# Three of the seven loads of the first double chunk issued from ScalarE's DMA queue

## The chip, the cores and the metric

The kernel runs on one core of a Trainium2 chip. The core has a matrix engine (TensorE, PE in the profile, with PEld for its weight loads), a vector engine (VectorE, DVE), an activation engine (ScalarE, ACT), a general engine (GpSimd, POOL) and a queue engine without arithmetic (SyncE, SP). Each takes its own instructions in program order and waits for the others on semaphores. Transfers between device memory and on-chip memory are issued by an engine's sequencer (SPq, ACTq, POOLq in the profile) and carried out by 16 DMA engines, which the core's queues share. The metric is device microseconds of one execution; lower is better.

## The reference

Two layers follow each other: a gated linear attention, and a feed-forward layer with a squared ReLU.

```python
batch, n_heads, seq, head_dim = (4, 8, 768, 48)     # q, k, v, alpha
n_tokens, d_model, d_ff = (3072, 384, 2048)
for t in range(S):
    state = alpha[:, :, t, :, None] * state + np.einsum('bhd,bhe->bhde', k[:, :, t], v[:, :, t])
    y[:, :, t] = np.einsum('bhd,bhde->bhe', q[:, :, t], state)
...
x = y.transpose(0, 2, 1, 3).reshape(B * S, H * D)
h = x @ w_in
r = np.maximum(h, 0.0)
return (r * r) @ w_out
```

All inputs and the output are float32.

## The kernel before

The 3072 tokens are 24 chunks of 128, six to a batch. For a chunk the attention is written with matrix products: the logarithm of alpha is summed along the chunk by a product with a triangular matrix, its exponentials A and 1/A (tiles `A` and `Ainv`) scale q and k, the scaled q and k are transposed, their product is masked and multiplied by v, and a running state (`st`, its copy `sb`) carries what earlier chunks left. The result `xn` is transposed into `xT_big`, from which the feed-forward layer reads: a first product (`w_in_b`), ReLU on ScalarE (`r`), square on VectorE (`gT`), a second product (`w_out_b`), copy and store.

The first four chunks are done as two double chunks (function `add_super`, u = 0 and 1), since they have nothing to hide behind. A double chunk reads `at` (alpha), `qt` and `kt` as two halves each, of four heads (`ld_at0`, `ld_at1` and so on, v = 0 and 1), and `vt` whole: seven loads, six of 192 KB and one of 384 KB. Function `add_load2` makes them. The first half of the heads goes through: logarithm (line 646, ScalarE), cumulative product p0 (PE), `A` and `Ainv` (line 682, ScalarE), the two scalings into `qk_s` (line 698, VectorE: q, then k), transposes p1 (line 276, PE), copy to `qkT` (line 396, VectorE), the masked scores `sm` (line 761, VectorE); the second half follows in the same way, and `vb` is the cast of `vt` (line 654, GpSimd). The state is advanced by the product `st` (PE) and its scaling at line 803 (VectorE).

The order of all instructions is made ahead of time, in the kernel's own Python: a class `Plan` lists operations with an engine, a duration and what they depend on, runs them through a list scheduler, and emits them sorted by start. Each engine then runs its own instructions in just this order. The loads are of the planner's kind "DMA"; the planner takes them one after another, LD2 = 1.51 us for a whole and half of it for a half load, starting at 0.8 us, with 2.0 us until the data count as there. Where PE would wait, the planner puts in matrix products of a constant tile (`warm`) that compute nothing that is used. They are part of the fixed order.

All loads of inputs and weights are issued by SyncE, in this order at the start:

```python
DMA_ORDER = ["0 at0 qt0 kt0 at1 qt1 kt1 vt", "1 at0 at1 qt0 kt0 qt1 kt1", "i", "1 vt"] + ["i"] * 5 + ["o"] * 4
```

Here "0" and "1" are the double chunks, "i" a part of w_in and "o" a part of w_out. GpSimd issues small transfers of the attention and most stores; ScalarE issues none. ScalarE's program begins with the load of its function table (line 213) and then the logarithm of `at0`.

Of the kernel before, what the change touches and what calls it, by code (L numbers as in the profile page):

```python
# [164 lines left out]
def kernel(  # L165
# [10 lines left out]
    nc = tc.nc  # L176
# [45 lines left out]
        out=utri_f, in_=ones_f, compare_op=ALU.is_ge, fill=0.0,  # L222
# [4 lines left out]
        out=sutri_f, in_=ones_f, compare_op=ALU.is_ge, fill=0.0,  # L227
# [9 lines left out]
    for src, dst in ((utri_f, half_in), (sutri_f, half_ex)):  # L237
        nc.vector.memset(dst, 0.0)
        for ab in range(2):
            h = slice(ab * HF, ab * HF + HF)  # L240
            nc.vector.tensor_copy(dst[h, h], src[h, h])
    for ab in range(2):
        h = slice(ab * HF, ab * HF + HF)
# [25 lines left out]
    def pin(ins):  # L269
        tc.keep_in_program_order(ins)  # L270
# [26 lines left out]
    def add(eng, dur, emit, *deps, **kw):  # L297
        return plan.add(Op(eng, dur, emit, deps, **kw))
# [77 lines left out]
    SRC2 = [("at", alpha), ("qt", q), ("kt", k), ("vt", v)]  # L376
    SRC2 = {n: x.rearrange("b h (u p s) d -> b u p h (s d)", p=P, s=2) for n, x in SRC2}

    HH = H // 2

    def add_load2(u, nm):
        d = SUP[u]
        nm, half = nm[:2], nm[2:]
        hs = slice(HH * int(half), HH * int(half) + HH) if half else slice(0, H)

        def ld():
            if nm not in d:
                d[nm] = loads.tile([P, H, 2, D], FP32, name=nm)
            pin(nc.sync.dma_start(out=d[nm][:, hs].rearrange("p h s d -> p h (s d)"), in_=SRC2[nm][0, u][:, hs]))  # L389
        d["ld_" + nm + half] = add("DMA", LD2 / 2 if half else LD2, ld, lat=2.0, at=0.8)  # L390

    def cast(op, out_t, in_t):
# [239 lines left out]
    def add_super(u):  # L632
# [9 lines left out]
        NH = NP // 2  # L642
        hsl = [slice(HH * v, HH * v + HH) for v in any_]

# [35 lines left out]
        def e_exp(v, nm, scale):  # L680
            d[nm][v] = work.tile([P, 2, HH, D], BF16, name="A" if nm == "A" else "Ainv")
            pin(nc.scalar.activation(d[nm][v], d["pm"][v][:, 0:HD].rearrange("p (t h d) -> p t h d", t=2, h=HH), AF.Exp,
                                     scale=scale))
# [381 lines left out]
```

## Time and profile before

| | |
|---|---|
| median of 3 runs | 181.26 us (180.81 to 181.36) |
| the profiled execution | 180.57 us |
| its span, first to last instruction | 178.9 us |
| granted TensorE clock | 1.00 |
| PE, DVE, ACT, POOL busy | 97%, 70%, 68%, 30% of the span |
| queue q1, which holds SyncE's transfers | 29.17 MB |
| queue q0, which holds GpSimd's transfers | 4.15 MB |

The profile was taken from one execution of the kernel as it runs otherwise. A time in it counts from the start of the span. A load has three times: the start of its issue on a sequencer, the duration of that issue, and the landing, when the waiting engine may read the data. A row of the timeline gives start, duration, engine, line, operation, output and inputs; a bracket gives the idle time of that engine ahead of it and what ended it.

### The profile page before, as it was taken

The numbers are of one execution on the slowest core, as the hardware profiler recorded it, in microseconds if no ns is written. First come the engines' busy times: TensorE is split into PE (matmuls) and PEld (weight loads), VectorE is DVE, ScalarE is ACT, GpSimd is POOL, SyncE is SP. The second block draws the span as 40 slices with busy tenths as digits, with TensorE's granted clock in tenths as the row PEclk, the third lists the DMA queues.
The fourth block names the chain that finished last, engine by engine and source line by source line (L and its number), as shares of the span: only waits on it lengthen the run. The fifth ranks groups of instructions, "written<-read, shape, count | busy, mean of one in ns | idle before, by whom it ended". The sixth has DMA issues, their size and how long they took to land.

```text
span 178.9 us, 4853 instructions
## 1 busy us (share of the span) xinstructions
PE 173.2 (97%) x1888; PEld 127.4 (71%) x1889; DVE 125.0 (70%) x262; ACT 122.4 (68%) x261; POOL 53.2 (30%) x95
## 2 busy tenths in 40 slices
PE   7899999999999999999999999999999999999993
PEld 2567585566897788878868767877867888668563
DVE  6699559736799798998986994975986748205100
ACT  4556689555998689979778927794893887328221
POOL 6021565721111212115033223256744640111100
DMA  5999899999989999999899997997986492221022
GB/s 144 271 275 322 268 346 376 235 208 205 218 174 186 200 196 196 205 178 212 166 218 195 206 208 149 205 205 137 230 216 176 113 234 88 48 88 44 0 88 92
DMA packets 112855, 33.63 MB, mean 188 GB/s; under 512 B 106896, under 2 KB 111120, under 8 KB 112832
## 3 DMA queue, kind: packets, MB, share of 16 engines
q1 hardware_dynamic: 110592, 29.17, 75.4%
q0 software_dynamic: 2240, 4.15, 8.2%
q8 instruction: 15, 0.25, 0.5%
q14 instruction: 8, 0.07, 0.1%
HBM read 25.17 MB, written 4.72 MB: 167 GB/s over the span
## 4 chain that ended last, share of the span: by engine, by line
PE 84%; SPq 5%; DMA 4%; ACT 2%; issue 1%; DVE 1%; POOL 1%; ACTq 0%
PE bank L273 76%; SPq L389 5%; DMA vt<-in_v_dram 4%; PE bank L276 4%; PE sc L273 2%; PE st L273 2%; ACT r L875 2%; POOL vb L654 1%; ACT xn L394 0%; DVE xT_big L396 0%; SPq L318 0%; DVE qk_s L494 0%; DVE qk_s L500 0%; ACT ob L911 0%; DVE gT L883 0%
## 5 line engine op out<-in xcount | busy, mean ns | idle before, releaser
L273 PE MATMUL bank<-xT_big,w_in_b 128*128 128x256 bf16 (+2 forms) x599 | 71.9, 268 | 0.2
L273 PE MATMUL bank<-w_out_b,gT 128*128 128x384 bf16 (+2 forms) x400 | 69.6, 319 | 0.0
L875 ACT ACTIVATE r<-bank 128x512 bf16<-128x512 f32 x96 | 56.3, 605 | 12.7 <-PE bank L273 10.5
L273 PEld LDWEIGHTS <-w_in_b 128*128 128x128 bf16 x600 | 53.0, 98 | 10.2 <-issue 0.3
L883 DVE TENSOR_TENSOR gT<-r 128x512 bf16<-128x512 bf16 x96 | 43.0, 479 | 16.5 <-ACT r L875 16.2
L273 PEld LDWEIGHTS <-gT 128*128 128x128 bf16 x400 | 36.9, 98 | 19.6 <-issue 0.2
L443 POOL CAST vb<-vt 128x384 bf16<-128x384 f32 x20 | 11.3, 570 | 52.1 <-DMA vt<-in_v_dram 24.0
L950 ACT COPY held<-bank 128x384 f32<-128x384 f32 x20 | 9.6, 480 | 17.8 <-PE bank L273 15.3
L483 POOL DMA_DIRECT2D ae_s<-Af x24 | 12.2, 513 | 21.8 <-ACT Af L466 19.9
L569 DVE TENSOR_TENSOR sm<-sc,utri_b 128x512 bf16<-128x512 f32 x24 | 15.4, 684 | 2.1 <-PE sc L273 2.1
L958 POOL DMA_DIRECT2D out_dram<-held x17 | 9.2, 547 | 22.4 <-ACT held L950 22.4
L394 ACT CAST xn<-bank 128x384 bf16<-128x384 f32 x24 | 11.1, 485 | 5.8 <-PE bank L273 5.6
L273 PEld LDWEIGHTS <-qkT 64*128 64x128 bf16 (+2 forms) x304 | 10.6, 97 | 5.2 <-issue 2.2
L497 DVE TENSOR_TENSOR qk_s<-qt,Af 128x384 bf16<-128x384 f32 x12 | 10.4, 863 | 4.4 <-ACT Af L466 4.0
L396 DVE COPY qkT<-bank 128x1024 bf16<-128x1024 bf16 (+1 forms) x16 | 9.7, 619 | 3.2 <-PE bank L276 3.2
L438 ACT ACTIVATE L_s<-at 128x384 bf16<-128x384 f32 x20 | 10.4, 528 | 2.1 <-DMA at<-in_alpha_dram 2.0
L466 ACT ACTIVATE Af<-bank 128x384 f32<-128x384 f32 x12 | 10.5, 873 | 1.8 <-PE bank L273 1.7
L500 DVE TENSOR_TENSOR qk_s<-kt,Ainv 128x384 bf16<-128x384 f32 x20 | 11.6, 581 | 0.0
L276 PE MATMUL bank<-ident_bf,qk_s 128*128 128x128 bf16 x112 | 10.2, 224 | 0.6 <-DVE qk_s L698 0.3
L603 DVE TENSOR_TENSOR st<-st,ae_s 128x384 f32<-128x384 f32 x16 | 8.9, 558 | 2.3 <-ACT xn L394 1.7
L470 ACT ACTIVATE Ainv<-bank 128x384 bf16<-128x384 f32 x20 | 10.3, 516 | 0.0
L569 DVE TENSOR_TENSOR sm<-bank,utri_b 128x512 bf16<-128x512 f32 x16 | 10.2, 683 | 0.0
(71 smaller groups left out, 168.4 us busy)
## 6 DMA issues: line engine op xcount, KB each, us to landing
at<-in_alpha_dram SPq DMA_DIRECT2D x24, 192.0 KB, 3.9
qt<-in_q_dram SPq DMA_DIRECT2D x24, 192.0 KB, 4.0
kt<-in_k_dram SPq DMA_DIRECT2D x24, 192.0 KB, 3.8
vt<-in_v_dram SPq DMA_DIRECT2D x20, 192.0 KB, 3.8
out_dram<-held POOLq DMA_DIRECT2D x17, 192.0 KB, 3.7
wo<-in_moe_w_out_dram SPq DMA_DIRECT2D x4, 768.0 KB, 7.7
wi<-in_moe_w_in_dram SPq DMA_DIRECT2D x4, 384.0 KB, 7.7
wi<-in_moe_w_in_dram SPq DMA_DIRECT2D x2, 768.0 KB, 5.5
```

The lines of the kernel that those rows point to most:

```text
L273: pin(nc.tensor.matmul(*a, **kw))
L276: pin(nc.tensor.transpose(*a))
L394: pin(nc.scalar.copy(out_t, in_t))
L438: pin(nc.scalar.activation(L[:, :, 0:D], d["at"], AF.Ln))
L443: pin(nc.gpsimd.tensor_copy(d["vb"], d["vt"]))
L466: pin(nc.scalar.activation(d["A"], split(d["pm"][:, 0:HD], s), AF.Exp))
L483: pin(nc.gpsimd.dma_start(out=ae_s[HF * j:HF * j + D, i, j], in_=d["Af"][P - 1:P, j]))
L497: pin(nc.vector.tensor_mul(qA[:, :, 0:D].rearrange(v4, j=2), d["qt"].rearrange(v4, j=2), d["A"]))
L500: pin(nc.vector.tensor_mul(kI[:, :, 0:D], d["kt"], d["Ai"]))
L569: pin(nc.vector.tensor_mul(d["sm"][:, hh], d["sc"][hh], utri_b.to_broadcast([P, NP, P])))
L875: pin(nc.scalar.activation(box["r"][:, 0:w], box["ph"][:, 0:w], AF.Relu))
L883: pin(nc.vector.tensor_mul(gT[g][:, f0:f0 + per, lo * P:lo * P + n], r, r))
```

## The change

Three of the seven loads of double chunk 0, `qt0`, `at1` and `kt1`, are issued by ScalarE instead of SyncE. Nothing else is edited; the planner still sees one stream of loads and gives the same order of instructions.

```diff
     HH = H // 2
+    ON_ACT = [(0, "qt0"), (0, "at1"), (0, "kt1")]
...
         def ld():
             if nm not in d:
                 d[nm] = loads.tile([P, H, 2, D], FP32, name=nm)
-            pin(nc.sync.dma_start(out=d[nm][:, hs].rearrange("p h s d -> p h (s d)"), in_=SRC2[nm][0, u][:, hs]))
+            q = nc.scalar if (u, nm + half) in ON_ACT else nc.sync
+            pin(q.dma_start(out=d[nm][:, hs].rearrange("p h s d -> p h (s d)"), in_=SRC2[nm][0, u][:, hs]))
```

## Prediction

> **What bounds the kernel now.** I began with the page's chain of work that ended last.
>
> ```profile
> PE 84%; SPq 5%; DMA 4%; ACT 2%; issue 1%; DVE 1%; POOL 1%; ACTq 0%
> ```
>
> PE holds the chain from 19.20 us to the end; before that the chain is SyncE's issues, then the landing of `vt` of double chunk 1 and its cast. So the change acts on the first 20 us only, and what it moves at the point where PE takes over goes one to one into the time, unless PE finds slack later; in the table of stages PE is busy 49.91 of the 50 us from 70 to 120, so I count none.
>
> The chain written out by time, at the hand-over:
>
> ```profile
> 10.76 7.37 DMA vt<-in_v_dram
> 18.18 0.97 POOL vb L654 x2
> 19.20 0.33 PE st L273 x4
> ```
>
> A chain names only the wait that came last, so I read the timeline of the first 20 us for the runner-up, engine by engine.
>
> ```profile
> 3.59 0.52 ACT L646 ACTIVATE L_s<-at 128x384 bf16<-128x384 f32 x1 [1.51 <-DMA at<-in_alpha_dram]
> 5.00 0.49 ACT L682 ACTIVATE A<-bank 128x384 bf16<-128x384 f32 x1 [0.89 <-PE bank L273]
> 5.39 0.48 ACT L682 ACTIVATE Ainv<-bank 128x384 bf16<-128x384 f32 x1
> 6.47 0.52 ACT L646 ACTIVATE L_s<-at 128x384 bf16<-128x384 f32 x1 [0.60 <-DMA at<-in_alpha_dram]
> ...
> 7.18 0.69 DVE L396 COPY qkT<-bank 128x1024 bf16<-128x1024 bf16 x1 [0.63 <-PE bank L276]
> 8.27 0.56 DVE L698 TENSOR_TENSOR qk_s<-qt,A 128x384 bf16<-128x384 f32 x1 [0.40 <-ACT A L682]
> ...
> 15.53 1.29 DVE L396 COPY qkT<-bank 128x1024 bf16<-128x1024 bf16 x2 [0.18 <-PE bank L276]
> ...
> 17.96 1.28 DVE L761 TENSOR_TENSOR sm<-bank,mask_EO 128x512 bf16<-128x512 f32 x2
> 19.63 0.57 DVE L803 TENSOR_TENSOR st<-st,ae_s 128x384 f32<-128x384 f32 x1 [0.39 <-PE st L273]
> ```
>
> The reader should see that from 8.27 to 19.24 us DVE works with one gap of 0.18 us, and that the gap is a wait for PE, which is itself in a dense run of transposes then. The front of this run is q's scaling of the second half at 8.27, and behind it `at1`, whose logarithm at 6.47 starts right as the data land. So the compute chain from `at0` and `at1` through DVE is only some tenths shorter than the chain through `vt`. That gap is the cover of everything below. PE's rows give it:
>
> ```profile
> 18.74 0.78 PE L273 MATMUL st<-vb,qk_s 64*128 64x96 bf16 x8 [0.30 <-POOL vb L654]
> ```
>
> with one more idle time, 0.17 us of PEld ahead of the first w_in product at 17.61 (ended by GpSimd's cast of w_in). Together 0.47 us: a chain late by more than that delays `st` at 18.74 and PE from there on.
>
> **What the DMA engines do.** The stages table (duration, busy time and count of PE, PEld, DVE, ACT, POOL, clock, DMA share, GB/s):
>
> ```profile
> 0.00:2.00 2.00, 0.94 (x3) 0.40 (x4) 0.56 (x8) 1.20 (x1) 1.37 (x9) 1.00 0.01 3
> 2.00:4.00 2.00, 2.00 (x6) 0.64 (x5) 1.91 (x6) 0.49 (x2) 1.41 (x5) 1.00 0.96 250
> 4.00:6.00 2.00, 1.94 (x8) 0.84 (x6) 1.40 (x10) 0.98 (x3) 0.00 (x0) 1.00 1.06 278
> ```
>
> They start at 2.0 us, some 1.2 us after the first issue at 0.81, and are full from there. They are not short of issues: an issue of 192 KB takes about 0.55 us from start to start (0.81, 1.33, 1.86, 2.41), that is 357 GB/s, against 250 to 278 moved; and from the eighth load on, SyncE's issue is held back (1.61 us at 4.61). Landings, from start of issue plus the time to landing of each: `at0` 0.81 + 2.8 = 3.6, `qt0` 4.6, `kt0` 5.7, `at1` 2.41 + 4.0 = 6.4, `qt1` 7.2, `kt1` 7.9, `vt` 9.45. I use these as a scale: the n-th half load moved lands at that time, whoever issued it.
>
> **The change, part by part.**
>
> Removed from SyncE: three issues of 0.55 us, 1.6 us. They bound nothing as long as the DMA engines are full, and the bytes ahead of `vt` of double chunk 1 stay the same, so I leave its landing at 18.13: gain 0. What hides the saving is the backlog of transfers; were it gone, the bounds are 0 and 3 x 0.72 us (the pace of SyncE's later issues, 7.81, 8.57, 9.29), of which only 0.47 us could show before DVE's run ends at 19.24.
>
> Added to ScalarE: three issues. The planner's times put `qt0` (1.56) and `at1` (3.07) ahead of the logarithm of `at0` (3.56), and `kt1` (4.58) between it and `A` (4.68). ScalarE idles there: 1.51 us before 3.59 and 0.89 before 5.00. Three issues of 0.55 us fit, cost 0. Behind `kt1`'s issue stand `A`, `Ainv` and the second logarithm; if that issue is held they wait (a rival below). The trace has no DMA issue on ScalarE, so its start is bounded: 0.85, with the other engines' first work, or 2.08, when the table load (0.80, 1.28 us) ends. I work out both.
>
> Moved, the order of the data. The trace shows no second load queue next to SyncE's. The nearest row is GpSimd's queue: `ae_s`, 0.8 KB, lands in 3.2 us at the median while SyncE's 192 KB loads take 3.9, so a second queue does not wait out the first one's backlog. The bounds are then: data served in order of issue (no change), and equal shares for both queues. I take equal shares, as that row is nearest to it.
>
> Early start, equal shares: from 2.0 us `at0` and `qt0` advance together, and `at0` is done when two halves have moved, so it lands at 4.63 instead of 3.61, +1.02. `kt0` and `at1` are done with the fourth half, 6.41, and `qt1` and `kt1` with the sixth, 7.90, all ahead of their use in the shifted chain. The logarithm, `A`, `Ainv`, both scalings and the transposes of the first half shift by 1.02, and the p0 product of the second half with them, since it stands behind those transposes on PE (7.04). So `qk_s` moves from 8.27 to 9.29.
>
> Late start, equal shares: ScalarE's data start at 2.08 + 1.2 = 3.3, when (3.3 - 2.0)/0.84 = 1.55 halves have moved (0.84 = (9.45 - 3.6)/7). `at0` is on time. `at1`, second on its queue, is done at 1.55 + 4 = 5.55, by the scale 7.57: +1.16 on the second logarithm, which starts right at its landing, and so on 8.27.
>
> Both starts give nearly the same, +1.02 and +1.16. DVE passes it on undiminished to 16.88, where PE waits for `qkT`; PE's 0.47 us of idle absorbs part, and `st` and all behind it come 0.55 to 0.69 late. The stalled work next in line, the ReLU at 18.48 and ScalarE's w_in cast at 19.23, moves by the same and delays SyncE's next weight issue, which has slack, as w_out is first used at 32.21. Sum: **+0.6 us**. The profiled execution, 180.57 with 1.67 around its span, becomes 181.2; the median shown is 0.69 above it, and I forecast 181.26 + 0.6 = **181.9 us**.
>
> On sharing, the Trainium skill (DMA: Bandwidth & Descriptors, Queues, rings and completion order) states that each DMA engine goes round between the queue rows that have work, a packet at a time; no run so far shows it for these two queues. By that rule the sum is the one above, by order of issue it would be nothing.
>
> **The rivals.**
>
> 1. *Order kept or delay absorbed.* If the queues are served in order of issue, or `at0` has moved most of its bytes before `qt0` joins, the shift at 8.27 is 0 to 0.4 and the 0.47 us swallow it: 181.3. For it: the new issue order alternates SP and ACT exactly as the old order ran. Against: at 2.0 us several issues of both queues are already waiting.
>
> 2. *The queues block each other's issues.* SyncE's ring fills sooner now, as its five halves of double chunk 0 go out by 2.9 us and double chunk 1 follows: its long issue (1.61 us at 4.61 before) would begin near 4.0. If `kt1`'s issue on ScalarE has to wait for it, it ends near 6.2, and `A` starts there instead of 5.00: +1.2; if SyncE's queue also drains at half its rate, the hold is 3.2 us and `A` comes near 7.7, +2.7. Less 0.47, between +0.7 and +2.2; I take +1.5: 182.8. For it: the hold is a row of the trace. Against: nothing shows that one queue's hold reaches another; GpSimd's transfers are of another kind. The Trainium skill (Perfetto Trace Analysis, Per-instruction lifecycle) says that a hardware-issued transfer locks the descriptor generator for its own use; no row here tests it.
>
> 3. *SyncE's issue is the bound after all.* The chain does run through SyncE's issues from 0.81 to 10.71. If the earlier issues bring `vt` of double chunk 1 forward by over 0.5 us, PE's 0.47 us go, and if the two queues together also fill the start better (the first halves land 1.02 apart, later ones 0.75), `at1` could come 0.3 earlier, into the 0.40 us that DVE idles before 8.27: -0.7 in all, 180.6. It decides only if `at0` is not late. Against: the full DMA engines, and 357 GB/s of issue. The Trainium skill's overview page (Trainium Kernel Development and Optimization, Key Constraints) says that several issuing engines save only the sequencer's time, which speaks against this rival.
>
> **How the numbers follow.** Forecast 181.9 (equal shares) 0.45, its own range 181.4 to 182.5; rival 2 at 182.8, 0.17; rival 1 at 181.3, 0.20; rival 3 at 180.6, 0.18. About 0.3%, 0.54 us, is what a measurement of this kernel can tell from no change. The forecast lies just outside, so a part of it (0.05) counts as same, and a part of rival 3 (0.03), whose first half alone is only -0.47. Slower 0.57, same 0.28, faster 0.15. The range goes from rival 3 to the upper part of rival 2: 180.6 to 183.1.
>
> **What would show it.** In the profile after: the first logarithm at 4.6 instead of 3.59 (early start), or the second near 7.6 instead of 6.47 (late start); q's scaling of the second half near 9.3; no idle left ahead of `st`, which starts near 19.3 instead of 18.74; `vt` of double chunk 1 landing near 18.1 still; GB/s from 2 to 8 us near 250 to 280 still. Rival 1 shows as 3.59, 6.47 and 8.27 unmoved; rival 2 as an issue of over 1 us on ACTq ahead of `A`; rival 3 as `vt` landing before 17.6. The prediction is wrong if the DMA engines move clearly more with two queues, or if PE gains or loses more than 0.3 us against its old order after 25 us.

## The result, and the profile after

The changed kernel takes 182.07 us, the median of 14 runs (181.51 to 185.07); the kernel before, run beside it on the same chip, 180.88 us (14 runs, 179.97 to 182.70). The ratio is 1.0074, its 95% interval 1.0051 to 1.0098: slower by about 1.3 us. It is taken over the faster executions alone; four of the changed kernel's, 184.27 to 185.07 us at a granted clock of 0.970 to 0.972, are not in it. The profiled execution took 182.04 us with a span of 180.2, against 180.57 and 178.9; the granted TensorE clock is 1.00 in both.

The page's chain of work that ended last now reads

```profile
PE 84%; DMA 5%; DVE 5%; ACT 3%; issue 2%; DVEq 0%; ACTq 0%
```

SyncE's issues (5%, the second entry before) are gone from it, and DVE rises from 1% to 5%: the change did what it says to SyncE, and another chain took over. The chain of the kernel after by time (start, duration, what) names it:

```profile
0.81 3.36 DMA at<-in_alpha_dram
4.17 0.02 issue
4.19 0.01 ACT L_s L648
4.20 5.62 DMA kt<-in_k_dram
...
9.91 0.06 DVE qk_s L700
9.97 0.41 issue
10.38 0.69 DVE sm L763
...
17.13 1.21 DVE qkT L398 x2
18.34 0.04 issue
18.38 1.39 PE bank L273 x26
```

Up to 18.4 us it is `at0`'s landing, the first logarithm, then `kt1`'s transfer, and from there DVE's work, piece upon piece. The surprising link is the third piece: a transfer from memory starts the moment an unrelated logarithm starts. The timeline of the kernel after shows why (line numbers past 380 are one or two higher than before; ACTq is ScalarE's sequencer):

```profile
0.84 0.47 ACTq L391 DMA_DIRECT2D qt<-in_q_dram  x1
1.34 0.57 ACTq L391 DMA_DIRECT2D at<-in_alpha_dram  x1
4.19 0.52 ACT L648 ACTIVATE L_s<-at 128x384 bf16<-128x384 f32 x1 [2.10 <-DMA at<-in_alpha_dram]
4.20 0.43 ACTq L391 DMA_DIRECT2D kt<-in_k_dram  x1
5.60 0.49 ACT L684 ACTIVATE A<-bank 128x384 bf16<-128x384 f32 x1 [0.89 <-PE bank L273]
...
9.23 0.56 DVE L700 TENSOR_TENSOR qk_s<-qt,A 128x384 bf16<-128x384 f32 x1 [0.66 <-ACT A L684]
9.91 0.56 DVE L700 TENSOR_TENSOR qk_s<-kt,Ainv 128x384 bf16<-128x384 f32 x1
...
14.77 0.89 POOL L322 CAST w_in_b<-wi 128x768 bf16<-128x768 f32 x1 [5.45 <-DMA wi<-in_moe_w_in_dram]
14.88 1.18 DVE L700 TENSOR_TENSOR qk_s<-qt,A 128x384 bf16<-128x384 f32 x1
...
25.20 0.36 DVE L398 COPY xT_big<-bank 128x384 bf16<-128x384 bf16 x1 [0.57 <-PE bank L276]
```

In the kernel before, the issue of `kt1`, k's scaling and the copy stood at

```profile
3.50 0.51 SPq L389 DMA_DIRECT2D kt<-in_k_dram  x1
8.75 0.55 DVE L698 TENSOR_TENSOR qk_s<-kt,Ainv 128x384 bf16<-128x384 f32 x1
...
24.22 0.36 DVE L396 COPY xT_big<-bank 128x384 bf16<-128x384 bf16 x1 [1.24 <-PE bank L276]
```

`kt1` stands behind the first logarithm in ScalarE's program, and that logarithm waits for `at0`. SyncE had issued `kt1` at 3.50, without any such wait; ScalarE issues it at 4.20, 0.01 us after the logarithm begins. The data, due at 7.9 before, are there at 4.20 + 5.62 = 9.82. The delay of the issue is only 0.70 us of these 1.9; the rest is that SyncE, rid of three loads, had meanwhile issued `vt` (2.40) and the first load of double chunk 1 (2.95), and their data went first (the packet counts further down show it). k's scaling of the second half starts at 9.91 instead of 8.75, 1.16 late, and the copy into `xT_big` for the fourth chunk, one of the last steps of the double chunks, at 25.20 instead of 24.22, 0.98 late.

PE's order is the same in both kernels, so a product group late in it can be compared directly. The score products `sc` that stand at 41.03 us before start 0.98 later after the change; the same groups at 55.4, 74.9 and 103.9 us start 0.98, 1.44 and 1.37 later, and the last, at 148.7, 1.37. So about three quarters of the loss is there at 41 us, and the rest is made between 55 and 75.

### The profile page after: what moved, and what is told of

Read it like the earlier page. It is cut to its first block, busy times and chain, and to the rows that moved or that the text cites. A ratio compares the mean times of both kernels' runs of the same rounds, so it can differ in the third digit from the quotient of the medians.

```text
span 180.2 us, 4853 instructions
## 1 busy us (share of the span) xinstructions
PE 174.0 (97%) x1888; PEld 128.0 (71%) x1889; DVE 128.1 (71%) x262; ACT 122.3 (68%) x261; POOL 54.3 (30%) x95
## 3 DMA queue, kind: packets, MB, share of 16 engines
q0 software_dynamic: 2240, 4.15, 8.0%
## 4 chain that ended last, share of the span: by engine, by line
PE 84%; DMA 5%; DVE 5%; ACT 3%; issue 2%; DVEq 0%; ACTq 0%
PE bank L273 76%; PE bank L276 4%; DMA kt<-in_k_dram 3%; PE sc L273 2%; ACT r L877 2%; PE st L273 2%; DMA at<-in_alpha_dram 2%; DVE sm L763 1%; DVE qk_s L700 1%; DVE qkT L398 1%; DVE xT_big L398 1%; ACT xn L396 0%; DVE st L805 0%; DVE qk_s L502 0%; DVE qk_s L496 0%
## 5 line engine op out<-in xcount | busy, mean ns | idle before, releaser
L885 DVE TENSOR_TENSOR gT<-r 128x512 bf16<-128x512 bf16 x96 | 45.3, 505 | 15.9 <-ACT r L877 15.6
L445 POOL CAST vb<-vt 128x384 bf16<-128x384 f32 x20 | 11.9, 600 | 53.5 <-DMA vt<-in_v_dram 25.9
L276 PEld LDWEIGHTS <-qk_s 128*128 128x128 bf16 x112 | 7.6, 100 | 3.8 <-DVE qk_s L700 1.6
L472 ACT ACTIVATE Ainv<-bank 128x384 bf16<-128x384 f32 x20 | 10.2, 512 | 0.0
```

The lines of the kernel that those rows point to most:

```text
L276: pin(nc.tensor.transpose(*a))
L445: pin(nc.gpsimd.tensor_copy(d["vb"], d["vt"]))
L885: pin(nc.vector.tensor_mul(gT[g][:, f0:f0 + per, lo * P:lo * P + n], r, r))
```

## The experiments

The theories as they stood. **Late kt1**: `kt1`'s issue is held by the semaphore wait of the logarithm ahead of it on ScalarE, and its landing sets DVE's run. **Late at0** (the forecast): `qt0` takes bandwidth from `at0`, and that delay is carried through the compute chain. **Half rate**: PE idles 0.54 us at 4.22 while it waits for the late logarithm, and then runs small products at half rate up to about 9.4 us (0.16 us apart instead of 0.08), which delays `A` of the second half. Twelve runs followed, on three chips, each against the kernel before on its own chip. There the kernel before ranged from 180.3 to 186.0 us (e), 182.1 to 188.2 (f) and 182.2 to 188.0 (g). Whole times of f and g therefore can't settle tenths of a per cent; the main evidence is the first 41 us of each profile, gathered here:

| kernel | ratio to before, 95% | 1st logarithm | q's, k's scaling, 2nd half | copy to `xT_big` | `sc` at 41.03 | last `sc` |
|---|---|---|---|---|---|---|
| before | | 3.59 | 8.27, 8.75 | 24.22 | 0 | 0 |
| f1, before again | 0.997 [0.989, 1.006] | 3.62 | 8.48, 8.96 | 23.90 | -0.32 | +5.12 |
| e1, `qt0` alone | 1.007 [1.003, 1.011] | 4.15 | 8.63, 9.11 | 24.05 | +0.21 | +1.28 |
| e2, `at1` alone | 1.004 [1.000, 1.007] | 4.16 | 8.33, 8.81 | 24.03 | -0.19 | +0.01 |
| g1, `qt0` and `at1` | 1.011 [1.003, 1.019] | 4.23 | 8.40, 8.88 | 24.09 | -0.13 | +3.19 |
| f3, all three, `kt1` early | 0.997 [0.989, 1.005] | 4.45 | 8.62, 9.09 | 24.29 | +0.08 | +4.16 |
| g2, f3 again | 1.013 [1.006, 1.020] | 4.36 | 8.54, 9.01 | 24.22 | +0.12 | +5.75 |
| after | 1.007 [1.005, 1.010] | 4.19 | 9.23, 9.91 | 25.20 | +0.98 | +1.37 |
| g4, after again | 1.001 [0.994, 1.008] | 4.40 | 9.44, 10.10 | 25.37 | +1.15 | +5.97 |
| f2, after again | 1.007 [1.000, 1.013] | 4.38 | 8.56, 10.10 | 28.40 | +4.18 | +4.34 |
| e3, `kt1` alone | 1.013 [1.007, 1.019] | 4.30 | 8.78, 9.73 | 24.95 | +0.74 | +5.70 |
| e4, one dummy more | 1.017 [1.012, 1.021] | 4.36 | 8.84, 10.07 | 25.53 | +1.31 | +3.93 |
| f4, w_in cast later | 1.017 [1.006, 1.028] | 4.36 | 9.40, 10.08 | 25.03 | +0.81 | +2.95 |
| g3, before, `kt1` late on SyncE | 1.026 [1.019, 1.033] | 3.62 | 8.03, 10.01 | 28.29 | +4.07 | +8.26 |

Times are us from the span's start; the last two columns are shifts against the first profile of before. f2 and g3 carry a second loss in this table, told in the last section.

**One load at a time (e1, e2, e3).** The list of ScalarE's loads is cut to one:

```diff
-    ON_ACT = [(0, "qt0"), (0, "at1"), (0, "kt1")]
+    ON_ACT = [(0, "qt0")]        # e1;  [(0, "at1")] in e2;  [(0, "kt1")] in e3
```

> Only qt0 is issued by ScalarE, the other two go back to SyncE. Theory (shared engines): qt0 takes a share of the DMA engines while at0 is moving, so the first logarithm stays near 4.2 us as with all three (3.59 before), PE idles about 0.5 us ahead of its first real product and does the following products at half rate, and q's scaling of the second half stays near 9.2 (8.27 before); kt1 lands near 8 as before, so k's scaling follows q's at once. Time 0.7 to 1.1 us over before. Rival (each issue on ScalarE costs its engine time): a third of the whole, about 0.4 us over before, with the first logarithm near 3.6.

> Only at1 is issued by ScalarE. Theory (shared engines): at1 takes the share that qt0 took, so the first logarithm is again near 4.2 us, with the same idle time of PE and the same slow products; time 0.7 to 1.1 us over before, though at1 itself lands earlier than before (6.41). Were at1's own landing what counts, the time would fall below before by up to 0.4 us. Rival (cost for each issue): about 0.4 us over before with the first logarithm near 3.6.

> Only kt1 is issued by ScalarE; its issue stands behind the first logarithm and so waits for at0. Theory: nothing shares with at0, first logarithm at 3.6 and PE without idle time ahead of its first product, issue of kt1 at 3.6, landing near 9 instead of 7.9, k's scaling of the second half late by 0 to 0.4 us; time within 0.3 us of before. Rival (cost for each issue): about 0.4 us over before.

`kt1` alone brings the late scaling back, `qt0` or `at1` alone does not. Each of the three expectations missed in part: with `qt0` alone q's scaling comes at 8.63, not near 9.2, with `at1` alone the time is 0.4% up, not 0.7 to 1.1 us, and with `kt1` alone the first logarithm is at 4.30, not 3.6, and the time 1.3% up, not within 0.3 us. The timeline of e3:

```profile
4.30 0.52 ACT L648 ACTIVATE L_s<-at 128x384 bf16<-128x384 f32 x1 [2.21 <-DMA at<-in_alpha_dram]
4.30 0.42 ACTq L391 DMA_DIRECT2D kt<-in_k_dram  x1
...
9.73 0.83 DVE L700 TENSOR_TENSOR qk_s<-kt,Ainv 128x384 bf16<-128x384 f32 x1 [0.40 <-DMA kt<-in_k_dram]
```

Here the bracket says it outright: DVE was idle 0.40 us, and `kt`'s transfer ended that. In the changed kernel no idle time shows at this place only because q's scaling was late too. Against the late-at0 theory, the first logarithm is as late in e1 and e2 (4.15, 4.16) as after the change (4.19), and yet their `xT_big` copy is at 24.05 and 24.03, no later than before. What e1's and e2's profiles don't explain is e1's whole time: it is 0.7% up, and of its 1.28 us at the end only 0.21 is there at 41 us; the rest comes in four places between 50 and 135 us. e2 ends level with before in its profile, and its interval, 0.9999 to 1.0071, just includes 1.

**PE's gap filled (e4).** One more dummy product where PE waits at 4.22:

```diff
-    idle_mm(7, 4)
+    idle_mm(8, 4)
```

> All three loads on ScalarE as in the changed kernel, and one more product of the constant tile (512 columns, about 0.43 us) after the seven at the start, to cover PE's idle 0.54 us from 4.22 to 4.76. Theory (the idle time leaves PE at half rate): the second half's cumulative products start 0.08 us apart instead of 0.16, A of the second half comes 0.7 us after the first of them instead of 1.07, q's scaling near 8.9 instead of 9.23; time 0.2 to 0.4 us below the changed kernel, still over before. Rival (the half rate has to do with the moment and not with the idle time): products still 0.16 us apart, time as the changed kernel.

The products of the second half do run at full rate. They start 0.08 us apart in the timeline of e4, the first two lines, and 0.16 us apart in that of the kernel after, the last two:

```profile
7.61 0.25 PE L273 MATMUL bank<-L_s,half_in 128*128 128x192 bf16 x1
7.69 0.25 PE L273 MATMUL bank<-L_s,half_ex 128*128 128x192 bf16 x1
...
7.64 0.36 PE L273 MATMUL bank<-L_s,half_in 128*128 128x192 bf16 x1
7.80 0.36 PE L273 MATMUL bank<-L_s,half_ex 128*128 128x192 bf16 x1
```

q's scaling comes at 8.84, earlier than after, but k's at 10.07, after 0.63 us of waiting for `kt`, and the copy at 25.53. The half rate was covered by `kt1`; no gain is seen from mending it alone. The cover is thin, though. In the changed kernel's own profile k's scaling would have come at 9.71 had `kt1` been in time (9.23 and 0.48 us, an estimate), against 9.91. The half rate at this place shows in three profiles, after, g4 and f4, all with a late `kt1`; e3, e4 and f2 show that a late `kt1` delays the scaling without it, but what it would cost with `kt1` in time no profile shows. That the gap causes the half rate is not shown: e1 and e3 have gaps of 0.50 and 0.65 us at the same place and their products are 0.08 us apart.

**kt1 ahead of the wait (f1, f2, f3, and again g1, g2, g4).** f1 and f2 are the two kernels unchanged, f3 sets ScalarE's issue of `kt1` right behind that of `at1`, ahead of the logarithm:

```diff
     plan.run(gate)
+    SUP[0]["ld_kt1"].start = SUP[0]["ld_at1"].start + 0.01
+    plan.order.sort(key=lambda o: o.start)
```

> The kernel before, looked at once more, as a control. The run with kt1 alone on ScalarE had its first logarithm at 4.30 although SyncE issued at0, qt0 and kt0 as before and ScalarE nothing ahead of 4.30. Theory A (the start of the transfers differs from execution to execution): this look shows the first logarithm anywhere from 3.6 to 4.3 us. Theory B (a second load queue slows the start of the transfers): it shows 3.6 again. Under both, k's scaling of the second half starts 0.48 us behind q's, without a wait for kt1, and the time is that of before within 0.3%.

> The changed kernel, looked at once more, next to the control. Theory A: the first logarithm varies as in the control; what stays is the wait for kt1 (k's scaling of the second half 0.7 to 1.3 us behind q's instead of 0.48) and the slow scaling on VectorE under GpSimd's cast of w_in. Theory B: the first logarithm at 4.2 again. Time 0.5 to 1% over before.

> As the changed kernel, but ScalarE issues kt1 right behind at1, ahead of the first logarithm, so that its issue does not stand behind the wait for at0. Theory (kt1's late issue is a main cost): issue near 1.9 instead of 4.2, landing near 7.5 instead of 9.8, k's scaling of the second half 0.48 us behind q's; 0.3 to 0.8 us below the changed kernel. Rival (the late first logarithm is the cost, kt1 is hidden behind it): no more than 0.2 us below the changed kernel.

The controls agree with theory B, first logarithms at 3.62 (f1) and 4.38 (f2); f2's k's scaling is 1.54 behind q's, more than foretold. In f3 the issue of `kt1` starts at 1.94, and k's scaling at 9.09 though the first logarithm is the latest of all, at 4.45; the copy is at 24.29. Nothing but the place of one issue differs in the program from f2 (10.10) and after (9.91). The ratio, 0.997, can't be told from 1, nor from the changed kernel's on that chip. g2 is the same program on the third chip, g4 the changed kernel, and g1 gives `kt1` back to SyncE (`ON_ACT` is `qt0` and `at1`):

> The changed kernel with one of its three loads undone: kt1 is issued by SyncE again, qt0 and at1 stay on ScalarE. Theory (the loss is kt1's issue, held behind the first logarithm's wait for at0): k's scaling of the second half follows q's 0.47 us behind, with no wait for a transfer; the copy of the fourth chunk into xT_big on VectorE between 23.9 and 24.4 us (24.22 before, 25.20 after the change); time within 0.3% of before. Rival (at0's late landing, about 4.2 instead of 3.6, is the loss): first logarithm late as in the changed kernel, copy near 24.8, time 0.3 to 0.6% over before.

> All three loads on ScalarE, kt1 issued ahead of the first logarithm, once more and beside the changed kernel on the same chip. Theory: as with kt1 back on SyncE, copy into xT_big between 23.9 and 24.4 us, time within 0.3% of before and 0.4 to 0.9% below the changed kernel. Rival: copy near 24.8, time as the changed kernel.

> The changed kernel, third look, beside the three others. Theory: kt1's issue starts with the first logarithm between 4.1 and 4.5, kt1 lands 5.3 to 5.7 us later, k's scaling of the second half starts then, copy into xT_big between 25.0 and 25.6, time 0.5 to 1% over before. Rival: k's scaling follows q's at 0.47 us in this execution and the loss is there all the same.

The first 41 us fall into the same two groups again, g1 and g2 at -0.13 and +0.12, g4 at +1.15. The timeline of g1, to be held against that of the kernel after:

```profile
2.40 0.51 SPq L391 DMA_DIRECT2D kt<-in_k_dram  x1
4.23 0.52 ACT L648 ACTIVATE L_s<-at 128x384 bf16<-128x384 f32 x1 [2.15 <-DMA at<-in_alpha_dram]
...
8.88 0.55 DVE L700 TENSOR_TENSOR qk_s<-kt,Ainv 128x384 bf16<-128x384 f32 x1
...
24.09 0.36 DVE L398 COPY xT_big<-bank 128x384 bf16<-128x384 bf16 x1 [1.24 <-PE bank L276]
```

The logarithm is as late as after the change, yet PE's 1.24 us of idle ahead of the copy is the same as before (0.57 after): this part of the chain has not moved. The whole times miss what was hoped of them. g1 and g2 measured 1.1% and 1.3% slower, g4, with the loss at 41 us, 0.1%, on a chip where the kernel before itself spreads over 5.8 us. What happens past 41 us differs from one execution to the next by more than the effect: the profile of f1, which is the kernel before, loses 4.5 us between 104 and 127 us, with PE idle 2.64 us on the transposing transfer into `xT_big`; f3, g1, g2, g4 and e3 wait there too (1.4 to 2.6 us). These whole times neither support nor refute the reading of the first 41 us.

**A late kt1 without a second queue (g3).** In the kernel before, SyncE issues `kt1` behind `at0` of double chunk 1:

```diff
     plan.run(gate)
+    SUP[0]["ld_kt1"].start = SUP[1]["ld_at0"].start + 0.01
+    plan.order.sort(key=lambda o: o.start)
```

> The kernel before, without any load on ScalarE, but SyncE issues kt1 three places later, behind vt and the first load of double chunk 1. By the landings of before it then lands near 10.2 us instead of 7.9. Theory (a late kt1 alone makes the loss): first logarithm near 3.6, k's scaling of the second half near 10.2 instead of 8.75, the copy into xT_big near 25.2 (1.5 us less the slack of about 0.5), time 0.4 to 0.8% over before. Rival (the loss needs the second queue): copy within 0.3 us of 24.22, time as before.

The timeline of g3:

```profile
3.62 0.52 ACT L646 ACTIVATE L_s<-at 128x384 bf16<-128x384 f32 x1 [1.54 <-DMA at<-in_alpha_dram]
5.34 0.55 SPq L389 DMA_DIRECT2D kt<-in_k_dram  x1
...
10.01 0.56 DVE L698 TENSOR_TENSOR qk_s<-kt,Ainv 128x384 bf16<-128x384 f32 x1 [1.42 <-DMA kt<-in_k_dram]
```

`at0` is on time, ScalarE issues nothing, and k's scaling is as late as in the changed kernel: a late `kt1` is enough for that. The copy comes at 28.29, not near 25.2, and it is the slowest kernel of all, 1.026; most of that shift goes with the clock, as told below, so g3 does not show the size of the loss.

**The cast beside the scaling (f4).** After the change w_in's first cast on GpSimd, at 14.77, lies beside q's scaling of double chunk 1, which takes 1.18 us instead of 0.55. f4 puts the cast behind that of `vt`:

```diff
     plan.run(gate)
+    w_ready["i"][0].start = SUP[1]["use_vt"].start + 0.01
+    plan.order.sort(key=lambda o: o.start)
```

> As the changed kernel, but GpSimd takes the two casts of vt of double chunk 1 ahead of its first cast of w_in, so that this cast no longer runs beside VectorE's scalings of q and k. Theory (the cast slows VectorE's scalings, whose inputs both lie in on-chip memory): no scaling of q or k near 15 us longer than 0.6 us unless a cast of vt runs beside it, the chain of VectorE earlier by 0.3 to 0.6 us at the masked scores of double chunk 1; the first w_in product may then wait for the later cast, so the time falls by 0 to 0.4 us. Rival (the long scaling comes from something else, a read of late data): it stays at 1.1 to 1.2 us.

The timeline of f4:

```profile
15.06 0.55 DVE L700 TENSOR_TENSOR qk_s<-qt,A 128x384 bf16<-128x384 f32 x1
...
17.46 0.82 POOL L322 CAST w_in_b<-wi 128x768 bf16<-128x768 f32 x1
```

With the cast out of the way the same scaling takes 0.55 us. The Trainium skill (SBUF — State Buffer, section SBUF: two separate sides) says that a VectorE operation with two inputs in SBUF and a GpSimd operation that reads SBUF hold one pair of ports in turn; 1.18 against 0.55 us agrees. k's scaling is 0.17 us later in f4 than after, the copy 0.17 earlier, so the collision is worth some 0.3 us, a third of what is lost at 41 us; e3 and f4, without it, lose 0.74 and 0.81 there, after, g4 and e4 0.98 to 1.31. With `kt1` in time there is a like one (k's scaling takes 1.08 or 1.09 us at about 15 us in e2, g1, f3 and g2), and nothing is lost there at 41 us. f4's whole time, 1.017 [1.006, 1.028], doesn't show the gain.

## Why the prediction came out right, and where it was wrong

**The outcome.** A time of 181.9 in a range of 180.6 to 183.1, slower at 0.57; measured 182.07. The median of before was 181.26 in the three runs shown and 180.88 in the fourteen behind the ratio, though, so the step of +0.6 us stands against about +1.3. The level came out closer than the step, by luck: the step was half of what came, and made of another delay. A sign came true by luck as well. q's scaling of the second half, foretold near 9.3, is at 9.23, but not because `at0` held up the second logarithm, which at 6.36 is earlier than before (6.47); it is late by the products at half rate (`A` at 8.71), and in f2, the same kernel without them, it is at 8.56.

**Added to ScalarE: "Three issues of 0.55 us fit, cost 0". This step failed.** I took the planner's place for `kt1`, between the logarithm and `A`, and saw idle time of ScalarE around it, but did not ask when its sequencer gets there: the instruction ahead waits for `at0`. Their durations, 0.43 to 0.57 us, were right, and the issue did not hold `A` up: its bracket still shows 0.89 us of idle, ended by PE. What was lost is the time until `kt1` is issued and then its place in the stream. With it failed that `qt1` and `kt1` are done at 7.90, "all ahead of their use in the shifted chain"; `kt1` landed at 9.8. In all six profiles in which the issue stands behind the logarithm the two start together (4.19 and 4.20, 4.30 and 4.30, 4.36 and 4.36, 4.36 and 4.37, 4.38 and 4.39, 4.40 and 4.41).

**Moved, equal shares: this step failed too; the data went in order of issue.** Of the two bounded starts the early one came (0.84, beside the table load). The packet records of the two queues (q1 is SyncE's, q10 ScalarE's), counted per 0.25 us from the first data packet at 1.93 us, look like sharing at the start:

```text
before  q1   94 152 186 169 184 190
after   q1  111  68  47 105 108  72  75 156
        q10   0   3  14  55 107 150 145  62
and from 6.93 us on
after   q1  171 177 175 156  94  23  18  82 151
        q10   0   0   0  19  81 152 158  93  25
```

There the two engines issue in turn, so that sharing and order of issue look nearly alike. `kt1` tells them apart. Its issue ends at 4.63 and the other packets of ScalarE's queue are done by 5.30, yet `kt1`'s first packet moves at 7.77, and its middle one when SyncE's queue has moved 5.97 half loads (of 528 packets each); those that SyncE had issued by then are six (`at0`, `kt0`, `qt1`, `vt` as two, `at0` of double chunk 1). The same count is 5.94 to 6.01 in g4, f2, e4 and f4, where again six were issued ahead, 6.93 in e3 with seven whose issue had ended, and 2.98 and 3.01 in f3 and g2 with three. So `kt1`, the sixth half load of before, became the ninth, with two of ScalarE's and six of SyncE's ahead of it. By the prediction's own scale the eighth lands at 9.45 and the ninth near 10.2, an estimate; it landed at 9.82. The order of issue was the bound that I did not take. By the round of the Trainium skill named in the prediction (DMA: Bandwidth & Descriptors, Queues, rings and completion order) `kt1` would have had its share of the packets as soon as they were in its queue; either the round was not kept or they came into the queue that late, which the records do not tell apart.

`at0` landed at 4.17 instead of 3.61, +0.56 where equal sharing gave +1.02, but sharing is not shown to be what delayed it. In e3 ScalarE's queue moves nothing before 6.91 us, and the first logarithm is at 4.30. All eleven profiles with a ScalarE queue have it at 4.15 or later, against 3.59, 3.62 and 3.62 in the three without. By 3.0 us both queues together had moved 316 to 548 packets in the eleven and 579 to 650 in the three, so the transfers as a whole start more slowly; why stays open. And the delay was not passed on "undiminished": q's scaling of the second half moved by 0.06 to 0.36 in e1, e2, g1, f3 and g2, since `at1` came sooner (second logarithm at 6.02 to 6.31, 6.47 before), which had set it. At 41 us nothing is left of it (-0.19 to +0.21).

**PE's idle 0.47 us as the cover: right, here.** k's scaling is 1.16 late, and the collision with w_in's cast adds some 0.3, so that the last masked scores start 1.50 late (17.96 before). `st` starts at 19.69 instead of 18.74, 0.95 late, its idle 0.30 gone: 0.55 us are absorbed. The two lines of the kernel after:

```profile
19.46 1.28 DVE L763 TENSOR_TENSOR sm<-bank,mask_EO 128x512 bf16<-128x512 f32 x2
19.69 0.51 PE L273 MATMUL st<-vb,qk_s 64*128 64x96 bf16 x8
```

The cover is not the same in every execution: in f1, the kernel before, `st` starts at 18.39 without idle time ahead of it.

**Removed from SyncE, gain 0: right in effect, wrong in the sign it named.** `vt` of double chunk 1 landed near 16.2, not "near 18.1 still". Rival 3 is right in that, though f1, the kernel before, has it near 17.2 already, within the sign that rival 3 named; but where `kt1` is in time too (e2, g1, f3, g2) the gain at 41 us is between 0.19 and -0.12, within what two profiles of before differ by (0.32). GB/s from 2 to 8 us are 248, 267 and 261, near what was said.

**The rivals.** Rival 1 (order kept or delay absorbed) fits the order of the data and, where `kt1` is in time, the shift of 0 to 0.4 that is absorbed; but `at0` is not unmoved, and ScalarE's wait changes the order itself, which it did not see. Rival 2 had the right symptom, a late issue on ScalarE, and the wrong holder: SyncE's and ScalarE's first issues ran side by side (0.81 to 1.27 and 0.84 to 1.31), so nothing here shows the lock of the descriptor generator that it named; the issue was held by its own engine's wait. The last sign of being wrong, PE gaining or losing more than 0.3 us after 25 us, also hits: +0.4 between 55 and 75 us after the change, with no cause shown.

**What is and isn't settled.** Shown: the late issue of `kt1` makes the loss of 0.7 to 1.3 us at 41 us; it comes and goes with that one issue, and in the changed kernel some 0.3 us of it come by way of the cast. Without ScalarE's queue, in g3, the late scaling is shown and the size of the loss is not. Not shown: what the half rate would cost with `kt1` in time, and that `kt1` in time brings the whole time back to that of before, since e1, g1 and g2 are slower as a whole, though level at 41 us. Open with it: the changed kernel's last 0.4 us, and what makes the transfers start more slowly with a second queue. No version is shown to beat the kernel before.

## What to carry to other kernels

A DMA issue that is moved to a compute engine takes over every wait of the instructions ahead of it there; so look not at that engine's idle time but at what its program waits for at the new place, and put the issue ahead of the first wait or leave it on a queue that has none. When a transfer becomes late, follow it to its own consumer, not only the transfer that you expected to be late. A load on a second queue did not get ahead of what the first queue had issued meanwhile, so count the loads issued before it on both queues. And with a second queue in the program the first load landed later (here by 0.6 us), which matters only if its chain is the one that ends last.

## What the runs showed of the hardware

- **The clock can drop after the wait for kt1.** In the profiles of f2 and g3 PE idles 1.14 and 1.58 us at the second half's transposes (0.82 at most in the other five with a late `kt1`), and the granted clock, 1.00 in the other twelve profiles up to 41 us, falls to 0.50 in the stages from 12 to 20 us, as the stages table of f2 shows (start and end, duration, busy time and count of PE, PEld, DVE, ACT, POOL, then the clock, DMA share and GB/s):

```profile
12.00:16.00 4.00, 3.95 (x57) 3.19 (x56) 3.14 (x5) 1.45 (x4) 0.83 (x1) 0.50 1.20 296
16.00:20.00 4.00, 4.00 (x47) 3.18 (x45) 2.56 (x6) 2.47 (x8) 1.68 (x3) 0.50 1.07 358
```

  This costs some 3 us (f2's shift at 41 us is 4.18, g4's 1.15). Both executions have a mean clock of 0.972 or 0.973 over the span. A mean of 0.970 to 0.973 appears in 10 of the 58 executions of kernels with a late `kt1` and in 1 of the other 121 whose clocks are listed; only the two profiles show where in the span it lies. So a late `kt1` may cost more on average than the ratios say. That the idle time causes the drop is not shown.
- **Loads of two queues moved in order of issue.** The middle packet of each load of ScalarE's queue moved when SyncE's queue had moved nearly as many half loads as it had issued ahead of it: 0.92 to 0.95 for one, 1.93 to 1.98 for two, 2.98 and 3.01 for three, 5.94 to 6.01 for six, 6.93 for seven.
- **Granted clock and rate can differ.** After the change products ran at 0.16 us apart up to about 9.4 us with a recorded clock of 1.00 (0.08 us apart in e4, at the same clock).
- **ScalarE's table load did not hold its DMA issues**: they started at 0.84 and 1.34 while the load ran (0.80 to 2.08).
